# The last layer by Strassen's scheme: low halves on VectorE, split first weights kept in DRAM, squares shared otherwise

## The chip, the cores and the metric

One core of a Trainium2 chip. The metric is the device time of one execution in microseconds, the median of several. Engines: PE (TensorE, matmul), DVE (VectorE), ACT (ScalarE), POOL (GpSimd); SP (SyncE) issues most DMAs, POOL the gathers.

## The reference

Linear attention feeds a mixture of experts, which feeds a last layer. Only the last layer is touched by the change: 2304 tokens of 512 features, 2048 hidden features, a squared relu between two matrices. Its weights come as 64-bit floats.

```python
def _moe2_ref(x, w_in, w_out):
    h = np.maximum(x @ w_in, 0.0)
    return (h * h @ w_out).astype(np.float32)

def reference(**kwargs):
    ...
    attn_out = _attn_ref(**attn_kwargs)
    x = np.ascontiguousarray(attn_out.transpose(0, 2, 1, 3)).reshape(B * S, H * D)
    x = _moe_ref(x=x, **moe_kwargs)
    return _moe2_ref(x=x, **moe2_kwargs)
```

## The kernel before

Instructions run on each engine in the order in which the code records them; a semaphore wait holds up whatever stands behind it on the same engine or queue.

**Split numbers.** A 32-bit operand is split into a high half (ACT copies it to the matmul's type `FR`) and a low half (operand minus high half), and a product is three matmuls: high by high, high by low, low by high.

**The last layer** runs over three blocks (`m`) of six tiles of 128 tokens, 768 tokens each. In a block it runs over 8 sets (`s`) of 256 hidden features; `u = 8 m + s` counts the sets from 0 to 23. In a set, `l_set`:

- The first matrix product is done by Strassen's scheme: tokens are cut in two halves of 384, hidden features in two halves of 128, the 512 inputs in two halves. Seven products (`product(u, p, ...)`, 6 matmuls each of 384 columns) take the place of eight. They use the seven combinations `wa` of the weights and seven combinations `xo` of the tokens. They go in turn into two PSUM banks, M0 and M1, in the order 1, 2, 6, 5, 7, 3, 4. `snap` (ACT) copies a bank to SBUF, `plus` (DVE) adds a snap and a bank, `relu` (ACT) does the last one. The results are c11, c22, c12 and c21, one for each pair of a hidden half `f` and a token half.
- `l_h(u, f, half, c)` makes relu, square and split of one of them into a tile `hq`: before the change relu on ACT (but for c21), the high half as a square on ACT, the full square and the low half on DVE (L1174, L1175).
- `l_2(u, f, half)` multiplies `hq` by the second weights `wo`: nine matmuls of 512 columns, accumulated over the sets of a block in six banks (N0, KV, Tk for token half 0; P, Tq, N1 for half 1). `l_2(u, 0, 0)` ends the set; the other three fill PE's time between the products of the next set (`gap`), so they use the `hq` of the set before.

**The weights.** `a_load` fetches 256 columns of the first weights into one buffer `wr` (512 KB); `a_sums` makes four sums of its quarters on DVE; `a_conv(u)` splits the seven combinations into `wa`: four copies on ACT, four subtractions, on POOL but for u = 0 (L1122). `wa` has two buffers, taken in turn. `o_load` and `o_conv` do the same for the second weights (two loads of 256 KB, L1129; two copies on ACT; two subtractions, on POOL but for u = 0, L1138). All this is done again for each block, though the weights are the same.

**The next block.** In sets 1 to 6 of a block the tokens of the next are made ready: `l_gather` (POOL, two gathers a tile, L1037), `l_sum` (ACT and DVE, L1044, L1045), `l_t` (four PE transposes into M1 within `l_2(u, 0, 0)`, then the ACT copy `xr`, L1056), `x_sum` (DVE, sets 5 to 7), `x_conv` (ACT copy and DVE subtraction of 768 columns; one in set 4, one in set 5, three in set 7, two in set 0).

**Outputs.** At a block's end six banks are copied by `l_out` (ACT, or DVE where `dve` is true) and stored by SP. Tiles n = 3 to 5 of token half 1 are kept back in `OUT` until the first set of the next block (set 8, set 16), where they are copied after the last two `l_h`; in set 9 and 17 the first `l_2` writes bank P again. The loads of the second weights for the next set stand behind these stores in SP's queue.

Of the kernel before, what the change touches and what calls it, by code (L numbers as in the profile page):

```python
# [9 lines left out]
FT = mybir.dt.float32  # L10
FR = mybir.dt.float32r
# [3 lines left out]
AF = mybir.ActivationFunctionType  # L15
# [17 lines left out]
def kernel(  # L33
# [928 lines left out]
    with ExitStack() as ectx:  # L962
# [3 lines left out]
        win_d = dram.tile([DM, F2], FT, name="win_d")  # L966
        wout_d = dram.tile([F2, DM], FT, name="wout_d")
        WIDE = {}

# [138 lines left out]
        def a_sums(u):  # L1108
# [4 lines left out]
            nc.vector.tensor_sub(s[:, 3], a12, s[:, 1])  # L1113

        def a_conv(u):
            a11, a12, a21, a22, s = a_parts(u)
            k = 2 + u % 2
            h, l = [wpb[0].tile([128, 7, 2, 128], FR, name="wa", tag=f"w{k}0{x}") for x in "hl"]
            for c, x in ((slice(0, 2), WR[u][:, :DC, :128].rearrange("p (i c) f -> p i c f", i=2)),
                         (2, a22), (slice(3, 5), s[:, :2]), (slice(5, 7), s[:, 2:])):  # L1120
                nc.scalar.activation(h[:, c], x, AF.Copy)  # L1121
                (nc.gpsimd if u else nc.vector).tensor_sub(l[:, c], x, h[:, c].bitcast(FT))  # L1122
            LW[u] = (h, l)
            del WR[u]
# [7 lines left out]
        def o_conv(u, f):  # L1132
            if f not in WB:
                WB[f] = wpb[0].tile([128, 2, 2, DM], FR, name="wo", tag="w21" + "hl"[f])
            t = WB[f][:, u % 2]
            r = WO[u, f]
            nc.scalar.activation(t[:, 0], r, AF.Copy)  # L1137
            (nc.gpsimd if u else nc.vector).tensor_sub(t[:, 1], r, t[:, 0].bitcast(FT))  # L1138
            WO[u, f] = t
# [25 lines left out]

        def l_h(u, f, half, c, done=False):
            if not done:
                nc.scalar.activation(c, c, AF.Relu)  # L1168
            if f not in HQ:
                pool, tag = ((wpb[0], "w31h"), (ep, "xtl"))[f]  # L1170
                HQ[f] = pool.tile([128, 2, 2, LH], FR, name="hq", tag=tag, bufs=1)
            q = HQ[f][:, half]
            nc.scalar.activation(q[:, 0], c, AF.Square)  # L1173
            nc.vector.tensor_mul(c, c, c)  # L1174
            nc.vector.tensor_sub(q[:, 1], c, q[:, 0].bitcast(FT))  # L1175
            HQ[u, f, half] = q
# [34 lines left out]
        def l_set(u, fill=()):  # L1211
# [19 lines left out]
            due = nxt is not None and 0 < s <= LB  # L1231
            b0, b1 = bank("M0", [128, LH]), bank("M1", [128, LH])
            product(u, 1, b0, True)
            s1 = snap(u, b0, "hh")
# [11 lines left out]
            steps([], [2])  # L1246
            if u + 1 < NU:
                a_sums(u + 1)
# [6 lines left out]
            steps([4], [6])  # L1255
            if u + 1 < NU:
                a_conv(u + 1)
# [13 lines left out]
            product(u, 4, b0, False)  # L1271
            c21 = relu(b0)
            l_h(u, 0, 1, c12)
            l_h(u, 1, 0, c21, True)
            if nxt is not None and s in (NSET - 4, NSET - 3):
                x_conv(nxt, s - NSET + 4)
            for t, n in OUT:
                l_out(t, n, n % 2)
            OUT.clear()
            if nxt is not None and s < LB:  # L1280
                l_gather(nxt * LB + s)
            l_2(u, 0, 0, (lambda: l_t(nxt * LB + s - 1, "M1")) if due else None)
            if u + 1 < NU:
                for f in range(2):
                    o_load(u + 1, f)
            if u + 2 < NU:
                a_load(u + 2)


# [58 lines left out]
        for pt in range(1, NP):  # L1348
# [3 lines left out]
            for f in range(NF):  # L1352
# [34 lines left out]
                if pt == NP - 1:  # L1387
# [17 lines left out]
                    if f == 5:  # L1405
                        x_conv(0, 0)
                        a_load(1)
                    if f == NF - 1:
                        x_conv(0, 4)
                        x_conv(0, 3)  # L1410
                        x_conv(0, 5)
# [112 lines left out]
```

## Time and profile before

| | |
|---|---|
| median of 3 executions | 1069.74 us (1069.7 to 1070.25) |
| the profiled execution | 1078.87 us |
| its span | 1077.0 us |
| mean granted clock of PE | 0.991 |
| last layer in the span | from about 662 us to the end |
| busy in the span | PE 1032.0, DVE 735.5, ACT 578.9, POOL 531.9 us |

Times in the rows are microseconds from the start of the span. A row of a timeline gives start, length, engine, line of the code, instruction, output and inputs by the program's names, shapes, how many were merged, and in brackets how long the engine had stood idle and what ended that. A matmul's end is modelled and overlaps the next one's start. The granted clock is a share of full speed.

### The profile page before, as it was taken

How to read it: one execution, taken by the hardware profiler on the slowest of the kernel's cores; microseconds unless marked ns; L12 is line 12 of the kernel's file. 1: busy time of each engine (PE TensorE's matmuls, PEld its weight loads, DVE VectorE, ACT ScalarE, POOL GpSimd, SP SyncE). 2: the span in 40 equal slices, each digit the busy share in tenths (PEclk: the TensorE clock that was granted, in tenths of full speed). 3: DMA queues.
4: the chain of work that ended last, by engine and by line, in shares of the span. 5: the costliest groups of instructions: out<-in, count | busy, mean ns of one | idle time of the engine just before them, and what ended most of it. 6: DMA issues, size and time to landing. Idle time of an engine off the chain costs nothing.

```text
span 1077.0 us, 19334 instructions
## 1 busy us (share of the span) xinstructions
PE 1032.0 (96%) x7180; PEld 887.6 (82%) x7180; DVE 735.5 (68%) x1434; ACT 578.9 (54%) x1206; POOL 531.9 (49%) x480
## 2 busy tenths in 40 slices
PE   7999999799999999999999999899998999989997
PEld 4776677688989898888898888798887898878996
DVE  5778798632677777786868737766785667866653
ACT  5887777225445353535344426656664655645552
POOL 3444556536546455554545332665555555445340
PEclk9999999899999999999999999999999999999999
DMA  5986533355556656565656342413204232132211
GB/s 148 288 216 204 182 119 111 119 178 186 160 192 199 198 176 206 170 208 184 197 174 203 132 129 82 164 61 117 98 20 158 98 118 70 49 120 76 79 40 61
DMA packets 119141, 153.09 MB, mean 142 GB/s; under 512 B 18306, under 2 KB 71682, under 8 KB 119042
## 3 DMA queue, kind: packets, MB, share of 16 engines
q1 hardware_dynamic: 113282, 132.92, 38.7%
q0 software_dynamic: 5760, 18.88, 5.0%
q8 instruction: 58, 0.95, 0.4%
q14 instruction: 41, 0.34, 0.1%
HBM read 109.22 MB, written 42.54 MB: 141 GB/s over the span
## 4 chain that ended last, share of the span: by engine, by line
PE 71%; DVE 15%; ACT 6%; issue 3%; DMA 2%; another core or an unknown queue 1%; SPq 0%; POOL 0%; ACTq 0%; DVEq 0%
PE M L101 29%; PE N L101 14%; PE KV L101 9%; PE Tq L101 5%; PE P L101 5%; PE Tk L101 3%; DVE c L1174 2%; PE kpair L101 2%; DVE xo L1094 1%; DMA wo<-wout_d 1%; DVE kd L435 1%; DVE kmx L433 1%; DVE c L1158 1%; ACT hq L1173 1%
## 5 line engine op out<-in xcount | busy, mean ns | idle before, releaser
L101 PE MATMUL M<-xo,wa 128*128 128x384 f32 x1008 | 197.0, 339 | 6.8 <-DVE c L1158 3.5
L101 PEld LDWEIGHTS M<-xo,wa 128*128 128x128 f32 x1008 | 178.8, 188 | 21.0 <-DVE c L1158 5.6
L236 ACT ACTIVATE hh<-M 128x304 fp32r<-128x304 f32 (+2 forms) x128 | 48.9, 422 | 225.3 <-PE M L101 204.7
L1122 POOL TENSOR_TENSOR wa<-wr,wa 128x512 fp32r<-128x512 f32 x92 | 117.3, 1305 | 84.7 <-ACT wa L1121 84.3
L1174 DVE TENSOR_TENSOR c<-c 128x384 f32<-128x384 f32 x96 | 76.3, 795 | 95.6 <-ACT hq L1173 95.6
L233 DVE SCALAR_TENSOR_TENSOR hl<-M,hh 128x304 fp32r<-128x304 f32 (+2 forms) x128 | 56.1, 470 | 125.1 <-ACT hh L236 121.6
L515 POOL PARTITION_ALL_REDUCE qmx<-ps x36 | 70.0, 1945 | 80.8 <-ACT ps L513 66.3
L1138 POOL TENSOR_TENSOR wo<-wo 128x512 fp32r<-128x512 f32 x46 | 60.8, 1343 | 94.4 <-ACT wo L1137 94.0
L101 PE MATMUL N<-wo,hq 128*128 128x512 f32 x288 | 83.0, 396 | 0.8 <-DVE hq L1175 0.8
L1175 DVE TENSOR_TENSOR hq<-c,hq 128x384 fp32r<-128x384 f32 x96 | 64.2, 669 | 3.3
L1168 ACT ACTIVATE c<-c 128x384 f32<-128x384 f32 x72 | 37.7, 523 | 50.7 <-DVE c L1158 50.7
L101 PEld LDWEIGHTS N<-wo,hq 128*128 128x128 f32 x288 | 54.0, 189 | 9.7 <-DVE hq L1175 1.2
L1153 ACT ACTIVATE snap<-M 128x384 f32<-128x384 f32 x72 | 34.7, 489 | 48.2 <-PE M L101 48.2
L1158 DVE TENSOR_TENSOR c<-M,snap 128x384 f32<-128x384 f32 x72 | 39.7, 551 | 28.3 <-PE M L101 20.9
L1121 ACT ACTIVATE wa<-wr 128x512 fp32r<-128x512 f32 x96 | 49.4, 569 | 15.8 <-DVE wr L1112 8.9
L1173 ACT ACTIVATE hq<-c 128x384 fp32r<-128x384 f32 x96 | 47.8, 521 | 2.3
L101 PE MATMUL N<-kvc,qp 128*64 128x81 f32 x1024 | 43.9, 238 | 3.9 <-issue 1.7
L101 PEld LDWEIGHTS N<-kvc,qp 128*64 128x64 f32 x1024 | 38.7, 138 | 8.1 <-issue 6.8
L101 PE MATMUL P<-wo,hq 128*128 128x512 f32 x144 | 41.7, 398 | 3.6 <-DVE o L1200 3.6
L1012 POOL TENSOR_TENSOR wx<-wx 128x256 f32<-128x256 f32 x32 | 23.6, 736 | 43.0 <-DVE wx L1008 43.0
L149 POOL TENSOR_TENSOR w30l<-wstage,w30h 128x512 fp32r<-128x512 f32 x16 | 22.7, 1420 | 41.1 <-ACT w30h L148 37.1
L1012 POOL TENSOR_TENSOR wd<-wd 128x256 f32<-128x256 f32 x32 | 23.6, 736 | 37.7 <-DVE wd L1008 37.7
(353 smaller groups left out, 2953.7 us busy)
## 6 DMA issues: line engine op xcount, KB each, us to landing
wstage<-in_moe_w_dram SPq DMA_DIRECT2D x128, 256.0 KB
wr<-win_d SPq DMA_DIRECT2D x24, 512.0 KB
wo<-wout_d SPq DMA_DIRECT2D x48, 256.0 KB
xg_d<-zero SPq DMA_DIRECT2D x8, 1216.0 KB
y_d<-y SPq DMA_DIRECT2D x32, 256.0 KB
wide<-in_moe_w_in_dram SPq DMA_DIRECT2D x32, 256.0 KB
wide<-in_moe_w_out_dram SPq DMA_DIRECT2D x32, 256.0 KB
xg<-xg_d SPq DMA_DIRECT2D x7, 768.0 KB
```

Source lines behind the costliest of these rows:

```text
L101: nc.tensor.matmul(o, l, r, start=start, stop=stop, skip_group_check=True)
L233: nc.vector.scalar_tensor_tensor(hl[:, c0:c1], o, 0.0, hh[:, c0:c1].bitcast(FT), op0=OP.max, op1=OP.subtract)
L236: nc.scalar.activation(hh[:, c[1]:c[2]], c[0], AF.Relu)
L515: nc.gpsimd.partition_all_reduce(mx, ps, 128, bass.bass_isa.ReduceOp.absmax)
L1012: nc.gpsimd.tensor_mul(part, part, exp)
L1121: nc.scalar.activation(h[:, c], x, AF.Copy)
L1122: (nc.gpsimd if u else nc.vector).tensor_sub(l[:, c], x, h[:, c].bitcast(FT))
L1138: (nc.gpsimd if u else nc.vector).tensor_sub(t[:, 1], r, t[:, 0].bitcast(FT))
L1158: nc.vector.tensor_add(c, o, t)
L1173: nc.scalar.activation(q[:, 0], c, AF.Square)
L1174: nc.vector.tensor_mul(c, c, c)
L1175: nc.vector.tensor_sub(q[:, 1], c, q[:, 0].bitcast(FT))
```

## The change

Five things change in the last layer:

- The low halves of both weights (`a_conv`, `o_conv`) are subtracted on DVE in every set; POOL has gathers alone.
- The split first weights of block 0 are stored: after the conversion of set u, SP writes both halves `wa` to a DRAM buffer `wa_d` (`a_store`). In blocks 1 and 2, `a_again` loads them back into the same two buffers; `a_load`, `a_sums` and `a_conv` are left out there.
- `l_h`: for c11 and c22 (`f == half`), ACT does relu, square and the copy to the high half, DVE the low half alone. For c12 and c21 DVE does relu and square in one instruction (max with 0, times c), ACT copies the high half, DVE subtracts.
- The kept-back outputs are copied before the last two `l_h` instead of after, P and N1 by ACT and Tq by DVE (before: P and N1 by DVE, Tq by ACT).
- c21, which is a relu already, goes through the same path as c12.

```diff
+        wa_d = dram.tile([F2 // 256, 2, 128, 7 * 256], FT, name="wa_d")
...
+        def a_tiles(u):
+            LW[u] = [wpb[0].tile([128, 7, 2, 128], FR, name="wa", tag=f"w{2 + u % 2}0{x}") for x in "hl"]
+            return LW[u]
+
+        def a_store(u):
+            for i in range(2):
+                nc.sync.dma_start(wa_d[u, i], LW[u][i].rearrange("p a c f -> p (a c f)").bitcast(FT))
+
+        def a_again(u):
+            for i, t in enumerate(a_tiles(u)):
+                nc.sync.dma_start(t.rearrange("p a c f -> p (a c f)").bitcast(FT), wa_d[u % NSET, i])
...
                 nc.scalar.activation(h[:, c], x, AF.Copy)
-                (nc.gpsimd if u else nc.vector).tensor_sub(l[:, c], x, h[:, c].bitcast(FT))
-            LW[u] = (h, l)
+                nc.vector.tensor_sub(l[:, c], x, h[:, c].bitcast(FT))
...
-            (nc.gpsimd if u else nc.vector).tensor_sub(t[:, 1], r, t[:, 0].bitcast(FT))
+            nc.vector.tensor_sub(t[:, 1], r, t[:, 0].bitcast(FT))
...
-        def l_h(u, f, half, c, done=False):
-            if not done:
-                nc.scalar.activation(c, c, AF.Relu)
+        def l_h(u, f, half, c):
...
             q = HQ[f][:, half]
-            nc.scalar.activation(q[:, 0], c, AF.Square)
-            nc.vector.tensor_mul(c, c, c)
+            if f == half:
+                nc.scalar.activation(c, c, AF.Relu)
+                nc.scalar.activation(c, c, AF.Square)
+            else:
+                nc.vector.scalar_tensor_tensor(c, c, 0.0, c, op0=OP.max, op1=OP.mult)
+            nc.scalar.activation(q[:, 0], c, AF.Copy)
             nc.vector.tensor_sub(q[:, 1], c, q[:, 0].bitcast(FT))
...
+            if NSET <= u + 1 < NU:
+                a_again(u + 1)
             product(u, 1, b0, True)
...
-            if u + 1 < NU:
+            if u + 1 < NSET:
                 a_sums(u + 1)
...
-            if u + 1 < NU:
+            if u + 1 < NSET:
                 a_conv(u + 1)
...
             c21 = relu(b0)
+            for t, n in OUT:
+                l_out(t, n, n % 2 == 0)
+            OUT.clear()
             l_h(u, 0, 1, c12)
-            l_h(u, 1, 0, c21, True)
+            l_h(u, 1, 0, c21)
...
-            for t, n in OUT:
-                l_out(t, n, n % 2)
-            OUT.clear()
...
-            if u + 2 < NU:
+            if u + 2 < NSET:
                 a_load(u + 2)
+            if u + 1 < NSET:
+                a_store(u + 1)
...
                         a_load(1)
+                        a_store(0)
```

DVE in set 2 (sets 1 and 3 read alike), from the weight sums of the next set to the squares of c12 and c21. In the names, `wr` is the raw first weight, `wa` its split form, `ya` a token tile of the next block, `M1` and `M0` the product banks. Before:

```order
L1110 TENSOR_TENSOR wr_8381<-wr_8381 128x256
L1111 TENSOR_TENSOR wr_8381<-wr_8381 128x256
L1112 TENSOR_TENSOR wr_8381<-wr_8381 128x256
L1113 TENSOR_TENSOR wr_8381<-wr_8381 128x256
L1045 SCALAR_TENSOR_TENSOR ya_8356<-yb_8357,gates_79,ya_8356 128x512
L1158 TENSOR_TENSOR c_8465<-M0_8383,snap_8436 128x384
L1174 TENSOR_TENSOR c_8465<-c_8465 128x384
L1175 TENSOR_TENSOR hq_8184<-c_8465,hq_8184 128x384
L1158 TENSOR_TENSOR c_8486<-M1_8384,snap_8428 128x384
L1174 TENSOR_TENSOR c_8486<-c_8486 128x384
L1175 TENSOR_TENSOR hq_8170<-c_8486,hq_8170 128x384
L1174 TENSOR_TENSOR c_8494<-c_8494 128x384
```

The same stretch of DVE now:

```order
L1114 TENSOR_TENSOR wr_8384<-wr_8384 128x256
L1046 SCALAR_TENSOR_TENSOR ya_8359<-yb_8360,gates_79,ya_8359 128x512
L1134 TENSOR_TENSOR wa_8446<-wr_8384,wa_8445 128x512
L1134 TENSOR_TENSOR wa_8446<-wr_8384,wa_8445 128x256
L1134 TENSOR_TENSOR wa_8446<-wr_8384,wa_8445 128x512 x2
L1169 TENSOR_TENSOR c_8470<-M0_8388,snap_8441 128x384
L1188 TENSOR_TENSOR hq_8186<-c_8470,hq_8186 128x384
L1169 TENSOR_TENSOR c_8491<-M1_8389,snap_8433 128x384
L1186 SCALAR_TENSOR_TENSOR c_8491<-c_8491 128x384
L1188 TENSOR_TENSOR hq_8172<-c_8491,hq_8172 128x384
L1186 SCALAR_TENSOR_TENSOR c_8499<-c_8499 128x384
L1188 TENSOR_TENSOR hq_8186<-c_8499,hq_8186 128x384
```

The four subtractions of `wa` stand ahead of the sum c22 (the first `c<-M0`); between c22 and c12 (`c<-M1`) the multiplication is gone; behind c12 a fused relu and square stands before each low half.

DVE at the seam of blocks 0 and 1, from c12 of set 8 to the first sum of set 9 (`o` is an output tile). Before:

```order
L1158 TENSOR_TENSOR c<-M_9267,snap 128x384
L1174 TENSOR_TENSOR c<-c 128x384
L1175 TENSOR_TENSOR hq<-c,hq 128x384
L1174 TENSOR_TENSOR c<-c 128x384
L1175 TENSOR_TENSOR hq<-c,hq 128x384
L1200 COPY o<-P 128x512
L1200 COPY o<-N_8263 128x512
L1158 TENSOR_TENSOR c<-M_9431,snap 128x384
```

And now:

```order
L1169 TENSOR_TENSOR c<-M_9262,snap 128x384
L1213 COPY o<-Tq 128x512
L1186 SCALAR_TENSOR_TENSOR c<-c 128x384
L1188 TENSOR_TENSOR hq<-c,hq 128x384
L1186 SCALAR_TENSOR_TENSOR c<-c 128x384
L1188 TENSOR_TENSOR hq<-c,hq 128x384
L1169 TENSOR_TENSOR c<-M_9413,snap 128x384
```

The copies of P and N1 have gone to ACT, directly behind the relu of c21, and the one copy left on DVE stands ahead of the squares.

SP's queue from the last loads of set 7 to those of set 10 (`wo` second weights, `wr` raw first weights, `wa_d` the DRAM buffer of split first weights). Before:

```order
L1129 DMA wo<-wout_d 128x512 x2
L1100 DMA wr<-win_d 128x4x256
L1209 DMA out_dram<-o 128x512 x6
L1129 DMA wo<-wout_d 128x512 x2
L1100 DMA wr<-win_d 128x4x256
L1129 DMA wo<-wout_d 128x512 x2
```

And now:

```order
L1122 DMA wa_d<-wa 128x1792 x2
L1126 DMA wa<-wa_d 128x1792 x2
L1140 DMA wo<-wout_d 128x512 x2
L1126 DMA wa<-wa_d 128x1792 x2
L1222 DMA out_dram<-o 128x512 x6
L1140 DMA wo<-wout_d 128x512 x2
L1126 DMA wa<-wa_d 128x1792 x2
L1140 DMA wo<-wout_d 128x512 x2
```

A reload of 1.84 MB (two DMAs) stands where a load of 0.5 MB stood; the second weights still stand behind the six outputs.

## Rows read from the trace of the kernel before

**Rows 1.** Page part 1: engine, busy us, share of the span, instructions.
```profile
PE 1032.0 (96%) x7180; PEld 887.6 (82%) x7180; DVE 735.5 (68%) x1434; ACT 578.9 (54%) x1206; POOL 531.9 (49%) x480
```

**Rows 2.** Waits of PE, 660 to 1077: total us, times, longest.
```profile
PE P L101 <- DVE o L1200: 3.6, 2, 1.8
```

**Rows 3.** Windows by set: length, busy PE, PEld, DVE, ACT, POOL, clock, DMA share, GB/s.
```profile
679.10:696.46 17.36, 16.67 (x84) 14.41 (x82) 12.31 (x17) 10.46 (x21) 11.87 (x10) 1.00 0.52 170
712.61:728.75 16.14, 16.14 (x84) 14.52 (x83) 9.79 (x17) 9.49 (x20) 9.48 (x8) 1.00 0.30 102
744.89:761.70 16.81, 16.64 (x83) 14.40 (x82) 13.00 (x21) 9.75 (x20) 9.71 (x8) 1.00 0.28 103
761.70:778.54 16.84, 16.52 (x83) 14.41 (x82) 13.12 (x22) 10.38 (x21) 8.25 (x6) 1.00 0.22 77
778.54:794.25 15.71, 15.71 (x79) 14.14 (x78) 14.03 (x20) 10.07 (x19) 8.69 (x6) 1.00 0.11 41
794.25:811.31 17.06, 16.46 (x79) 13.96 (x78) 13.35 (x20) 11.14 (x22) 8.46 (x6) 1.00 0.22 77
811.31:833.93 22.62, 18.73 (x83) 15.38 (x82) 11.54 (x20) 10.61 (x22) 11.40 (x10) 0.92 0.43 141
948.80:968.76 19.96, 16.49 (x80) 13.91 (x78) 10.75 (x18) 8.70 (x18) 7.48 (x6) 1.00 0.36 119
815.38:819.00 3.62, 3.62 (x9) 2.80 (x10) 1.01 (x2) 0.00 (x0) 0.85 (x1) 0.57 0.71 241
```

**Rows 4.** Timeline of set 3: start, us, engine, line, what [idle before].
```profile
720.22 0.75 DVE L1045 SCALAR_TENSOR_TENSOR ya<-yb,gates,ya 128x512 f32<-128x512 f32 x1 [0.23 <-ACT ya L1044]
720.78 4.86 POOL L1122 TENSOR_TENSOR wa<-wr,wa 128x512 fp32r<-128x512 f32 x4 [3.27 <-ACT wa L1121]
722.24 0.56 DVE L1158 TENSOR_TENSOR c<-M,snap 128x384 f32<-128x384 f32 x1 [1.26 <-PE M L101]
723.38 0.53 ACT L1173 ACTIVATE hq<-c 128x384 fp32r<-128x384 f32 x1
724.54 1.52 DVE L1175 TENSOR_TENSOR hq<-c,hq 128x384 fp32r<-128x384 f32 x1
725.98 0.54 DVE L1158 TENSOR_TENSOR c<-M,snap 128x384 f32<-128x384 f32 x1
727.36 0.94 ACT L1173 ACTIVATE hq<-c 128x384 fp32r<-128x384 f32 x2
728.24 0.60 ACT L1056 ACTIVATE xr<-M 128x512 f32<-128x512 f32 x1
```

**Rows 5.** By line, last layer: count, ns min/median/max, first and last start.
```profile
L1174 DVE TENSOR_TENSOR c<-c x96: 544/559/2331, 674.6 to 1063.9; 128x384 f32<-128x384 f32 x96
L1122 DVE TENSOR_TENSOR wa<-wr,wa x4: 418/684/691, 651.7 to 653.3; 128x512 fp32r<-128x512 f32 x3, 128x256 fp32r<-128x256 f32 x1
```

**Rows 6.** Timeline of the seam between blocks 0 and 1, columns as before.
```profile
814.65 0.68 DVE L1200 COPY o<-P 128x512 f32<-128x512 f32 x1
816.71 1.05 SPq L1129 DMA_DIRECT2D wo<-wout_d  x2
818.15 0.95 POOL L1037 DMA_INDIRECT ya<-y_d,yrows  x1 [8.25 <-DMA out_dram<-o]
820.04 0.63 ACT L1137 ACTIVATE wo<-wo 128x512 fp32r<-128x512 f32 x1 [6.27 <-DMA wo<-wout_d]
822.22 0.63 ACT L1137 ACTIVATE wo<-wo 128x512 fp32r<-128x512 f32 x1 [1.55 <-DMA wo<-wout_d]
823.73 0.86 ACT L1153 ACTIVATE snap<-M 128x384 f32<-128x384 f32 x2
825.23 0.72 ACT L1044 ACTIVATE ya<-ya,gates 128x512 f32<-128x512 f32 x1 [0.65 <-DMA ya<-y_d,yrows]
```

**Rows 7.** Timeline of PE, set 6: product 2 waits.
```profile
763.26 1.31 PE L101 MATMUL M<-xo,wa 128*128 128x384 f32 x6 [0.32 <-ACT xr L1056]
```

**Rows 8.** A window of 2 us at the start of set 2, columns as in rows 3.
```profile
696.00:698.00 2.00, 2.00 (x12) 1.91 (x11) 1.58 (x3) 1.50 (x4) 0.00 (x0) 1.00 1.05 374
```

More of the change, by code (lines that the diff above doesn't have):

```diff
@@ L1113, in a_sums @@
             nc.vector.tensor_sub(s[:, 3], a12, s[:, 1])
+        def a_tiles(u):
[7 more added lines that the diff above has]
+                nc.sync.dma_start(t.rearrange("p a c f -> p (a c f)").bitcast(FT), wa_d[u % NSET, i])
         def a_conv(u):
             a11, a12, a21, a22, s = a_parts(u)
-            k = 2 + u % 2
-            h, l = [wpb[0].tile([128, 7, 2, 128], FR, name="wa", tag=f"w{k}0{x}") for x in "hl"]
+            h, l = a_tiles(u)
             for c, x in ((slice(0, 2), WR[u][:, :DC, :128].rearrange("p (i c) f -> p i c f", i=2)),
```

## The prediction

> **What bounds the kernel now.** I read the page first: TensorE (PE) is busy for 96% of the span [rows 1], so the end can move only where PE waits. The waits of the last layer come next: PE waits there, twice for 1.8 us, for an output copy of VectorE (DVE) [rows 2]. The third view cuts the last layer at the first matmul of each set [rows 3]; it carries the argument. There are 24 sets, 8 for each of three blocks of tokens. An undisturbed set lasts 16.14 us where it carries four transposes for the next block (sets 1 to 6 and 9 to 14) and 15.71 us elsewhere. What exceeds that is lost: 1.22 us in set 1, 0.67 and 0.70 in sets 5 and 6, 1.35 in set 8, 6.48 in set 9, 4.25 in set 17. Sets 13, 14 and 16 repeat 5, 6 and 8 to a hundredth or two. Together that is 10.4 + 4.25 + 2.7 = 17.4 us, the most that this change can win. The other sets lose nothing worth a row, so faster helpers win nothing in them.
>
> Why sets lose: in set 3 (no loss) one subtraction of DVE takes 1.52 us and ends 0.42 us after the group of four on GpSimd (POOL), which ends at 725.64 [rows 4]; instructions of this size have a median of 0.56 and a longest of 2.33 [rows 5]. So DVE is held up while POOL works. At the seam from block 0 to block 1, PE waits until DVE has copied bank P at 815.33, since the copies stand behind four squares and subtractions; SyncE (SP) issues the next second weights only behind the last output, at 816.71; ScalarE (ACT) stands before their conversion until 820.04 and again until 822.22, and the snap that frees PE's bank starts at 823.73 [rows 6]. After PE's wait of 1.80 us the granted clock is 0.57 over 3.62 us [rows 3], between the upper level (2.4 GHz) and the lower (1.2 GHz): 3.62 x 0.43 = 1.6 us more.
>
> **The change part by part.** *POOL's subtractions leave.* Then DVE's instructions of 384 columns stay at 0.56 us. In set 3 that takes 1.52 - 0.56 = 0.96 us out between the sum c22 (722.24) and the sum c12 (725.98) [rows 4].
>
> *They go to DVE.* The second weights' two (0.68 us each, as in [rows 5]) fall where DVE waits for ACT's chain on c11; their cover is that DVE is busy 9.79 of 16.14 us [rows 3]. The first weights' four cost 3 x 0.684 + 0.418 = 2.47 us [rows 5], in sets 0 to 6 only, and stand just ahead of c22. There DVE idled 1.26 us [rows 4], and neighbours overlap by some 0.1 (two squares take 0.94 us, not twice 0.53), so c22 comes 0.8 us later (bounds 0.4 and 1.2). With the 0.96 won, c12 comes at 725.8, as good as before.
>
> *The chain behind c12.* Before: two squares on ACT, end 728.30, then the copy `xr` that frees bank M1 [rows 4]. Now DVE squares c12, ACT copies, DVE subtracts, DVE squares c21, ACT copies, in this order, and `xr` stands behind the second copy. With 0.56 for each of DVE's four steps, 0.53 for the copies, 0.03 for a hand-over (722.24 + 0.56 and so on to 723.38) and 0.60 for `xr`, less overlaps, `xr` ends 3.8 us after c12's sum starts: 729.55. Set 4 starts at 728.75 and its product 2 wants M1 1.05 later, at 729.80. Slack 0.25 us. The fused square has no row; its nearest are 0.56, a product of 384 columns [rows 5], and 0.75, a fused one of 512 [rows 4]. I take 0.56 for the size; at 0.75 the slack is gone.
>
> Where ACT has a conversion of 768 columns (some 0.8 us) between, in sets 4 and 5, `xr` is 0.75 later; in sets 5 and 6 DVE also has four block sums of 256 columns (0.42 each [rows 5]) ahead of c22. Product 2 then waits 0.5 us in set 5, 1.2 in set 6 and 0.5 in set 7. Each wait also costs PE a restart: with 0.32 of waiting [rows 7] set 6 lost 0.70, part of it elsewhere; I add 0.2. Sum 2.8 us against 1.37 now. Set 1, where second weights and gather land late and a store of 1.84 MB is new in the queue, loses 1.5 against 1.22. Set 0 gains a subtraction at 0.56 and pays the four on DVE: zero, between -0.8 and +0.6.
>
> *Blocks 1 and 2 load the split weights.* Gone from each set: four sums, four ACT copies, the four subtractions. c22 has nothing ahead of it, c12 starts as product 3 ends, and `xr` has 0.5 us of slack; behind a conversion it misses by 0.2. Sets 13 and 14 lose 0.4 each instead of 0.7. Each set reloads 2 x 128 x 1792 x 4 bytes = 1.84 MB. SP issues it as soon as the products of the set before are through, so it has a set's length. The queue moved 374 GB/s in a full stretch [rows 8]: 5 us. In set 1 it moved 170: 11 us [rows 3]. Both fit; I price it at zero. Behind SP's wait for PE stand only the second weights, due a set later.
>
> *The seams.* The three held-back outputs come ahead of the last two squares, P on ACT. Product 4 ends some 13.7 us into set 8 (15.71 less nine matmuls, 3.62 x 0.57); after the relu of c21 and one copy, 0.6 us or so each, P is free at 14.9, ahead of PE's need in set 9: the wait of 1.80 us is gone, and the clock's 1.6 with it. SP issues the second weights at 16.3 instead of 22.5 us after set 8's start; with 3.33 us to land [rows 6] ACT starts 3.9 us into set 9, the second 2.2 later at worst, and with relu, square and copy the snap is taken at 8.8; product 7 wants it at 8.4. That loses 0.4, and as much again if the gather (issued at 818.15, landed at 825.23; now issued near 812) holds up the sum ahead of c22: set 9 loses 0.8, set 17, without a gather, 0.3. Sets 8 and 16 lose nothing: DVE has no weight sums and no stretched subtractions there.
>
> On this gather: before, it landed 7.1 us after its issue with 1 MB of weights beside it; now 1.84 MB stand in SP's queue before it. In order of issue it would wait 5 us or more for them, and set 9 would lose 3 to 4; no row here tells whether it does. The Trainium skill (DMA: Bandwidth & Descriptors, "Queues, rings and completion order") states that each DMA engine alternates between the queue rows it has work for; by that the gather shares and set 9 stays near 0.8.
>
> **Sum.** Now 17.4. After: set 1 1.5, sets 5 to 7 2.8, set 9 0.8, sets 13 and 14 0.8, set 17 0.3, together 6.2. Gain 11.2 us of the profiled 1078.87, that is 1.04%; of the median 1069.74 that leaves **1058.6 us**. The profiled execution is 0.9% above the median; I assume that waits scale with it.
>
> **The rivals.** *B, the longer chain:* `xr` is half a microsecond later than summed. Then sets 3 and 4 wait too (0.45 each), the four late ones of block 0 and three of block 1 wait 0.5 more: +4.4, **1063**. For it: a slack of 0.25. Against: nearly every part has a row.
>
> *C, the seam half mended:* the 1.80 waits go, but weights or gather land as late as before, behind six outputs and the reload: set 9 keeps 6.48 - 1.80 - 1.6 = 3.1, set 17 2.45: +4.5, **1063**, up to 1066 with the gather in order of issue.
>
> *E, DVE is not held up by POOL:* then the 0.96 stays, and c12 costs some 0.9 us in six sets of block 0 and 0.6 in six of block 1: +9, **1068**, not to be told from no change. Against: the long subtraction ends with POOL's group. The Trainium skill (GPSIMD Engine Reference, "Specifications") says that POOL shares its SBUF interfaces with DVE and contends with instructions of two SBUF inputs; the trace agrees (2.33 us at most against 0.56).
>
> *D, slower:* the reloads miss their set. A set of block 1 moves 1.84 + 0.52 (second weights) + 0.52 (gather) = 2.88 MB in 16.14 us, so below 178 GB/s PE waits at product 1. At 155 GB/s, between sets 1 and 9 (170 and 141 [rows 3]), each of 8 sets would take 18.6 us: +19.6 - 11.2, **1078**. It outweighs the gain below 163 GB/s. Against: those sets had less to move, and 374 was reached.
>
> **How the numbers follow.** Forecast 0.62 (own spread 1054 to 1061.5: all but 1.5 us of the loss won at best, the slack gone at worst), B 0.16, C 0.14, E 0.04, D 0.04. Range 1053.5 to 1065: it takes in B and most of C and leaves out E, D and the tails. A measurement of this kernel tells 0.2% (2.1 us): faster 0.92, same 0.04, slower 0.04.
>
> **What would show it.** Right: no arithmetic on POOL in the last layer, DVE's 384 columns at 0.56 throughout, sets 8 and 16 at 15.7, set 9 near 17, set 17 near 16, no wait of PE for an output copy, waits for `xr` in sets 5 to 7. B shows as waits for `xr` in sets 3 and 4, C as ACT idle for second weights over 3 us, D as PE waiting for the reload. Wrong altogether if sets that lose nothing now lengthen.

## Result and profile after

The changed kernel takes 1060.6 us (median of 4 runs, 1059.99 to 1061.37), the kernel before 1069.72 (4 runs, 1068.85 to 1070.25). The ratio is 0.9916, with a 95% interval from 0.9899 to 0.9933: 9.1 us or 0.85% faster. The forecast was 1058.6, in a range from 1053.5 to 1065.

The profiled execution took 1060.74 us, with a span of 1059.0. The page's line of busy times, which answers to [rows 1]:

```profile
PE 1024.3 (97%) x7180; PEld 884.9 (84%) x7180; DVE 672.9 (64%) x1394; ACT 563.8 (53%) x1168; POOL 352.9 (33%) x342
```

DVE, ACT and POOL all have less to do. The waits of PE from 640 us on answer to [rows 2]; the columns after the colon are the sum, the count and the longest:

```profile
PE M L101 <- ACT xr L1057: 3.9, 7, 1.0
PE M L101 <- DVE c L1169: 1.9, 1, 1.9
PE Tk L1055 <- DVE ya L1046: 0.3, 1, 0.3
```

Before, beside the 3.6 us for the output copies, the larger waits were:

```profile
PE M L101 <- DVE c L1158: 3.5, 8, 1.3
PE M L101 <- ACT snap L1153: 2.3, 2, 1.5
PE M L101 <- ACT xr L1056: 0.7, 2, 0.3
```

No output copy is among the waits now: both of 1.8 us at the seams are gone, and so are those for a snap and all but one for a sum c. In their place stand seven waits for `xr`, the copy that frees bank M1, where there were two. Where they fall is read from the windows by set, which answer to [rows 3] (set 0, 1, 2, 4, 5, 6, 8, 9, 10 and 17; the number behind the stretch is its length, the third from the end the granted clock):

```profile
653.28:671.00 17.72, 15.66 (x72) 13.47 (x71) 15.24 (x27) 13.99 (x26) 0.00 (x0) 0.90 0.26 83
671.00:687.60 16.60, 16.58 (x84) 14.41 (x82) 9.45 (x20) 9.70 (x19) 6.50 (x7) 1.00 0.87 324
687.60:704.85 17.25, 16.42 (x84) 14.48 (x83) 11.23 (x22) 10.26 (x21) 1.90 (x3) 1.00 0.59 227
720.98:737.12 16.14, 16.14 (x83) 14.52 (x82) 10.28 (x20) 10.17 (x21) 1.63 (x2) 1.00 0.57 214
737.12:753.92 16.80, 16.42 (x83) 14.48 (x82) 12.31 (x25) 10.61 (x21) 0.00 (x0) 1.00 0.43 157
753.92:771.41 17.49, 16.45 (x84) 14.49 (x83) 12.78 (x26) 10.80 (x21) 0.00 (x0) 1.00 0.56 214
787.70:803.40 15.70, 15.70 (x79) 14.14 (x78) 7.73 (x14) 10.80 (x20) 0.00 (x0) 1.00 0.39 155
803.40:820.27 16.87, 16.84 (x84) 14.32 (x82) 7.14 (x14) 8.11 (x16) 6.26 (x7) 1.00 0.95 341
820.27:837.52 17.25, 16.42 (x84) 14.48 (x82) 7.84 (x14) 8.41 (x17) 1.89 (x3) 1.00 0.42 162
934.56:950.27 15.71, 15.71 (x80) 14.14 (x78) 7.44 (x14) 7.39 (x15) 0.00 (x0) 1.00 0.70 248
```

Sets 8 and 17 lose nothing, set 9 0.73 instead of 6.48. Sets 2 and 10, which lost nothing before, lose 1.11 each, sets 5 and 6 0.66 and 1.34, and set 0 is 1.12 longer. The table gives all kernels of this study, one profiled execution of each: the length of set 0, and for the others what they lose over 16.14 or 15.71 us (sets left out lose under 0.3). Each number is worked out from the starts of the sets in that kernel's trace. The last column is the time from the start of set 0 to the end. Up to 1.5 us of set 0 is chance (last section).

| kernel | set 0 | 1, 2 | 5 to 7 | 8 | 9 | 10 | 13 to 15 | 16 | 17 | 0 to end |
|---|---|---|---|---|---|---|---|---|---|---|
| before | 16.60 | 1.23 | 1.37 | 1.35 | 6.48 | 0 | 1.38 | 1.36 | 4.25 | 414.5 |
| before_again | 16.61 | 0.95 | 1.37 | 1.34 | 6.59 | 0 | 1.36 | 1.36 | 4.33 | 414.3 |
| changed | 17.72 | 1.57 | 2.59 | 0 | 0.73 | 1.11 | 1.07 | 0 | 0 | 405.7 |
| after_again | 16.16 | 3.02 | 2.58 | 0 | 0.05 | 1.13 | 1.04 | 0 | 0.09 | 404.8 |
| only_low_on_dve | 17.72 | 0 | 0.16 | 0 | 5.90 | 0 | 0.16 | 0 | 5.06 | 409.6 |
| lows_and_outputs | 17.62 | 0.09 | 0.14 | 0 | 1.24 | 0 | 0.15 | 0 | 0 | 400.1 |
| outputs_behind | 17.71 | 1.30 | 2.58 | 0 | 4.52 | 1.13 | 1.04 | 0 | 5.81 | 414.8 |
| no_reload | 17.70 | 0 | 2.58 | 0.06 | 1.01 | 1.11 | 2.59 | 0.06 | 0.24 | 406.2 |
| squares_paired | 16.14 | 1.99 | 0.17 | 0 | 0 | 0 | 0 | 0 | 0 | 399.1 |
| sum_behind_c22 | 17.69 | 1.03 | 1.17 | 0 | 0 | 0 | 1.04 | 0 | 0 | 401.6 |
| three_edits | 15.88 | 2.85 | 0 | 0 | 0 | 0 | 0 | 0 | 0 | 399.0 |
| old_squares_sum_behind | 16.16 | 0 | 0 | 0 | 0.44 | 0 | 0 | 0 | 0.28 | 397.6 |
| old_squares_set0_pool | 16.59 | 0 | 0 | 0 | 0.93 | 0 | 0 | 0 | 0.25 | 398.0 |
| paired_no_reload | 17.69 | 0 | 0 | 0 | 0.62 | 0 | 0 | 0 | 0 | 399.1 |

The kernel before took 1069.6 us beside the first four experiments and 1079 beside the other eight. Times are therefore compared as ratios within a group, and columns of the last layer across groups.

### The profile page after: what moved, and what is told of

Its sections match the earlier page's. It is cut to its first block, busy times and chain, and to the rows that moved or that the text cites. A ratio compares the mean times of both kernels' runs of the same rounds, so it can differ in the third digit from the quotient of the medians.

```text
span 1059.0 us, 19130 instructions
## 1 busy us (share of the span) xinstructions
PE 1024.3 (97%) x7180; PEld 884.9 (84%) x7180; DVE 672.9 (64%) x1394; ACT 563.8 (53%) x1168; POOL 352.9 (33%) x342
## 4 chain that ended last, share of the span: by engine, by line
PE 77%; DVE 11%; ACT 6%; DMA 3%; issue 1%; SPq 0%; POOL 0%; DVEq 0%; ACTq 0%; POOLq 0%
PE M L101 32%; PE N L101 15%; PE KV L101 9%; PE Tq L101 6%; PE P L101 6%; PE Tk L101 3%; DMA yb<-y_d,yrows 2%; PE kpair L101 2%; DVE kd L435 1%; ACT hq L1187 1%; DVE kmx L433 1%; DVE wa L1134 1%; DVE hq L1188 1%; PE qpair L101 1%; PE M L207 1%
## 5 line engine op out<-in xcount | busy, mean ns | idle before, releaser
L1188 DVE TENSOR_TENSOR hq<-c,hq 128x384 fp32r<-128x384 f32 x96 | 53.6, 559 | 86.3 <-ACT hq L1187 86.3
L1038 POOL DMA_INDIRECT ya<-y_d,yrows x18 | 18.4, 1024 | 194.5 <-PE M L101 82.7
L1187 ACT ACTIVATE hq<-c 128x384 fp32r<-128x384 f32 x96 | 50.3, 524 | 34.8 <-DVE c L1186 33.2
L1183 ACT ACTIVATE c<-c 128x384 f32<-128x384 f32 x48 | 25.2, 524 | 60.6 <-DVE c L1169 60.6
L101 PE MATMUL Tk<-wo,hq 128*128 128x512 f32 x144 | 42.1, 400 | 0.0
L101 PE MATMUL KV<-wo,hq 128*128 128x512 f32 x144 | 41.3, 395 | 0.0
L101 PE MATMUL Tq<-wo,hq 128*128 128x512 f32 x144 | 40.9, 392 | 0.0
L776 POOL DMA_INDIRECT xg_d<-x,slots x32 | 33.1, 1035 | 12.1 <-issue 4.8
```

Source lines behind the costliest of these rows:

```text
L101: nc.tensor.matmul(o, l, r, start=start, stop=stop, skip_group_check=True)
L776: st = nc.gpsimd.indirect_dma_start(out=xg_d, out_offset=bass.IndirectOffsetOnAxis(ap=slots[:, T0[g] + i, c:c + 1], axis=0), in_=src, in_o ...
L1038: nc.gpsimd.indirect_dma_start(out=y, out_offset=None, in_=y_d[:YA_ROWS] if t < LB else y_d, in_offset=bass.IndirectOffsetOnAxis(ap=yrows[ ...
L1187: nc.scalar.activation(q[:, 0], c, AF.Copy)
```

## Is the gain in the last layer?

The two first profiles stand 18 us apart, the medians 9. So the kernel before was profiled again, unchanged.

> The kernel before, unchanged. My theory: the 9 us by which the profiled execution of the kernel before stood above its median lay ahead of the last layer (there set 0 began at 662.5 us, in the changed kernel at 653.3) and were chance; then set 0 begins near 653.5 here, the profile's span is near 1068, the last layer to the start of the last second-layer stretch takes 400.8 again, and the losses by set are those of the first profile to 0.2 us each. Rival: the change also shortens the stretch ahead of the last layer; then set 0 begins at 662 again and the median is near 1078. The time against itself: 1069.7, ratio 1.000 within 0.2%.

Measured: 1069.92 us, ratio 1.0007 (0.9998 to 1.0017). Set 0 began at 653.16, the span was 1067.5, and the last layer lost what it had lost before (table). The extra 9 us of the first profile lie ahead of it, nearly all around one stretch; the first row is the first profile of the kernel before, the second the one taken again:

```profile
204.00:224.00 20.00, 15.66 (x92) 13.99 (x91) 8.89 (x53) 1.34 (x5) 11.25 (x21) 0.83 0.43 155
```
```profile
204.00:224.00 20.00, 18.77 (x122) 16.37 (x121) 9.93 (x49) 4.62 (x13) 9.86 (x19) 1.00 0.51 178
```

In the first, PE ran 92 matmuls there at a granted clock of 0.83, in the second 122 at 1.00, the upper level. "Chance" was not the whole of it: in each later group all seven runs of the kernel before lay near 1079, so this is a level that can hold for a whole group, and the first profile was taken on it. The groups also ran on three different chips, so whether the level goes with the chip stays open. The last layer is the same on both: 414.5 and 414.3 us. The changed kernel's 405.7 and 404.8 say that the gain, 9.2 us on the mean, is all there.

## One part alone: the low halves on DVE

```diff
-                (nc.gpsimd if u else nc.vector).tensor_sub(l[:, c], x, h[:, c].bitcast(FT))
+                nc.vector.tensor_sub(l[:, c], x, h[:, c].bitcast(FT))
...
-            (nc.gpsimd if u else nc.vector).tensor_sub(t[:, 1], r, t[:, 0].bitcast(FT))
+            nc.vector.tensor_sub(t[:, 1], r, t[:, 0].bitcast(FT))
```

> The kernel before with one part of the change alone: all low halves of the first and second weights on VectorE, none on GpSimd. My theory (GpSimd's arithmetic held VectorE up): the subtractions of 384 columns fall from 0.67 to 0.56 us on the mean, none is over 1 us, which pays for the four subtractions of weights (2.5 us a set) now ahead of c22; sets 5, 6, 13, 14 keep their 0.7 each, the seams keep 6.5 and 4.3: 1069.7, between 1067 and 1072. Rival E (VectorE isn't held up by GpSimd): the mean stays at 0.67 and c12 comes 0.8 us later in the sets of the first two blocks; the slack of the old chain takes part of it: 1073 or more.

Measured: 1064.55 us, ratio 0.9942 (0.9919 to 0.9964): 5 us faster, outside what I had expected and on the other side of rival E. DVE's subtraction of 384 columns, in the kernel before (first row) and here (second row; minimum, median and longest in ns):

```profile
L1175 DVE TENSOR_TENSOR hq<-c,hq x96: 557/558/1532, 666.5 to 1055.1; 128x384 fp32r<-128x384 f32 x96
```
```profile
L1175 DVE TENSOR_TENSOR hq<-c,hq x96: 557/558/565, 666.7 to 1050.1; 128x384 fp32r<-128x384 f32 x96
```

No stretched instruction is left (the longest multiplication fell from 2.33 to 0.61 us), so rival E falls: POOL's arithmetic did hold DVE up. And sets 1, 5, 6, 8, 13, 14 and 16 give back nearly all that they lost, 6.4 us by the table, though DVE has more to do (in set 3 it is busy 11.34 us instead of 9.79). The seams keep 5.9 and 5.1. The Trainium skill (GPSIMD Engine Reference, "Specifications") says that POOL contends with DVE's instructions of two SBUF inputs; the rows agree, and show how far: 1.53 us against 0.56.

## One part undone: the order of the outputs

```diff
-            for t, n in OUT:
-                l_out(t, n, n % 2 == 0)
-            OUT.clear()
             l_h(u, 0, 1, c12)
             l_h(u, 1, 0, c21)
             if nxt is not None and s in (NSET - 4, NSET - 3):
                 x_conv(nxt, s - NSET + 4)
+            for t, n in OUT:
+                l_out(t, n, n % 2)
+            OUT.clear()
```

> The changed kernel with one part undone: the held-back output copies stand again behind the last two squares of the set, with the old share of the engines. My theory (the order of the copies is what mended the seams): PE waits for an output copy again, 1.8 us at each seam, the granted clock falls behind each wait, and the second weights are asked for 6 us later; set 9 loses 6 us or so, set 17 4.2: 1060.6 + 5.6 + 4.2 = 1070, between 1067 and 1071. Rival: the seams were mended because GpSimd, the block sums and the conversions left them; then the order is worth little, set 9 loses under 3 us and set 17 under 1.5, and the time is below 1064.

Measured: 1070.59 us, ratio to the kernel before 1.0005 (0.9996 to 1.0015): without the order, nothing is left of the gain. Its waits of PE from 650 us on:

```profile
PE M L101 <- ACT snap L1164: 5.3, 2, 2.9
PE M L101 <- ACT xr L1057: 3.9, 7, 1.0
PE M L101 <- DVE c L1169: 2.1, 2, 1.9
PE P L101 <- DVE o L1213: 1.9, 2, 0.9
```

The waits for the output copy are 0.9 here, not 1.8, as with the low halves alone (1.0); the larger part, 5.3, is the snap behind the late second weights. So the order works through two routes, as the prediction had it, and the second is the dearer one. Sets 9 and 17 lose 4.52 and 5.81 here, 0.73 and 0 with the order. Of the granted clock, which I had expected to fall behind each wait, only set 17 shows a fall (0.92; set 9 1.00).

## One part undone: store and reload

All three blocks load and split the plain weights; `a_store` and `a_again` are not called.

```diff
-            if NSET <= u + 1 < NU:
-                a_again(u + 1)
...
-            if u + 1 < NSET:
+            if u + 1 < NU:
                 a_sums(u + 1)
...
-            if u + 1 < NSET:
+            if u + 1 < NU:
                 a_conv(u + 1)
...
-            if u + 2 < NSET:
+            if u + 2 < NU:
                 a_load(u + 2)
-            if u + 1 < NSET:
-                a_store(u + 1)
...
-                        a_store(0)
```

> The changed kernel with one part undone: nothing of the split first weights is stored or reloaded; all three blocks load the plain weights, form the block sums and split them, on ScalarE and VectorE. My theory: sets 13 and 14 lose 2.6 together with set 15 as sets 5 to 7 do now, instead of 1.1, and the sums and conversions stand ahead of c22 in sets 8 to 22 as well; against it set 1 may win 0.4 without the store, and the gathers of block 1 share the DMA queues with less, so sets 9 and 10 lose 1 us instead of 1.8: 1062, between 1060.5 and 1065. Rival (the reload costs as much as it saves, because the gather waits beside it): no difference from 1060.6 or faster, with sets 9 and 10 under 1 us.

Measured: 1060.36 us, ratio to the kernel before 0.9919 (0.9896 to 0.9942), no difference from the changed kernel's 1060.6, the rival's time. But the sum is made of two parts that cancel. Sets 1, 2 and 13 to 15 here:

```profile
670.56:686.71 16.15, 16.15 (x84) 14.53 (x83) 10.42 (x21) 9.88 (x20) 6.02 (x7) 1.00 0.69 219
686.71:702.85 16.14, 16.14 (x84) 14.52 (x83) 10.28 (x20) 10.18 (x21) 1.89 (x3) 1.00 0.31 98
868.14:884.94 16.80, 16.42 (x84) 14.48 (x82) 12.32 (x25) 10.61 (x21) 0.00 (x0) 1.00 0.19 63
884.94:902.40 17.46, 16.42 (x83) 14.49 (x82) 12.74 (x26) 10.80 (x21) 0.00 (x0) 1.00 0.18 61
902.40:918.72 16.32, 16.00 (x79) 14.11 (x78) 12.67 (x24) 11.02 (x21) 0.00 (x0) 1.00 0.10 32
```

Sets 13 to 15 lose 2.59, as sets 5 to 7 do, instead of 1.07: the reload saves 1.5 there. Sets 1 and 2 lose nothing instead of 1.57: the store costs that. With it in the queue the gather of set 1 lands late, and DVE, which sums the gathered rows ahead of c22, stands still. In the changed kernel's set 1:

```profile
680.26 0.75 DVE L1046 SCALAR_TENSOR_TENSOR ya<-yb,gates,ya 128x512 f32<-128x512 f32 x1 [2.56 <-DMA yb<-y_d,yrows]
680.93 2.22 DVE L1134 TENSOR_TENSOR wa<-wr,wa 128x512 fp32r<-128x512 f32 x4
683.07 0.55 DVE L1169 TENSOR_TENSOR c<-M,snap 128x384 f32<-128x384 f32 x1
```

Sets 9 and 10 lose 1.01 and 1.11 here, where I had expected 1 us together and the rival less. The gather is in time (DVE starts its sum at 811.27 without having waited for it), but the four subtractions of first weights, 2.22 us, now stand ahead of c22 in its place. So the loss at the seam is not the reload's alone.

## Two parts without the new squares

The kernel before with the low halves on DVE (diff above) and

```diff
             c21 = relu(b0)
+            for t, n in OUT:
+                l_out(t, n, n % 2 == 0)
+            OUT.clear()
             l_h(u, 0, 1, c12)
             l_h(u, 1, 0, c21, True)
             if nxt is not None and s in (NSET - 4, NSET - 3):
                 x_conv(nxt, s - NSET + 4)
-            for t, n in OUT:
-                l_out(t, n, n % 2)
-            OUT.clear()
```

> The kernel before with two parts of the change: all low halves on VectorE, and the held-back output copies ahead of the last two squares; the squares stay shared as before, nothing is reloaded. My theory (the new sharing of the squares lengthens the chain to the copy that frees bank M1 and costs some 5 us, the reload is worth nothing): the losses are those of the kernel with the low halves alone but with the seams mended: set 0 1.1 more than before, sets 6 and 14 0.2 each, sets 9 and 17 1 and 0.3 instead of 5.9 and 5.1: 1054.5, between 1053 and 1057, which beats the changed kernel by 6 us. Rival (the outputs can come first only because the new squares take ScalarE's two squares at the end of the set away): here c21's and c12's squares hold up product 1's snap, sets 9 and 17 lose 3 us each: 1059 or more.

Measured: ratio 0.9866 (0.9849 to 0.9882) to the kernel before, 1065.09 us where that took 1079.12; 400.1 us from set 0 to the end, 5.6 less than the changed kernel. It is well ahead of the changed kernel, whose ratio was 0.9916 and later 0.9919. So one part of the change, the new sharing of the squares, costs some 6 us: 406.2 without the reload against 400.1, two kernels that differ in the squares alone.

## The chain behind c12, and the sum ahead of c22

The first kernel changes the order within the last two squares alone; what it replaces are the two calls of `l_h`, which did square, copy and subtraction one after the other for c12 and then for c21.

```diff
-            l_h(u, 0, 1, c12)
-            l_h(u, 1, 0, c21)
+            pair = []
+            for f, half, c in ((0, 1, c12), (1, 0, c21)):
...
+                nc.vector.scalar_tensor_tensor(c, c, 0.0, c, op0=OP.max, op1=OP.mult)
+                nc.scalar.activation(q[:, 0], c, AF.Copy)
+                pair.append((q, c))
+            for q, c in pair:
+                nc.vector.tensor_sub(q[:, 1], c, q[:, 0].bitcast(FT))
```

> The changed kernel with the steps behind c12 and c21 in another order: both fused squares of VectorE first, then both copies of ScalarE, then both subtractions, so the copy that frees bank M1 comes about 1.06 us earlier (0.55 of a square and 0.59 of waiting drop out). My theory (that copy is late, and it alone costs sets 2, 5 to 7, 10, 13 and 14): their waits for it, 3.9 us in all, and the 0.2 that each adds go: sets 5 to 7 and 13 to 14 lose under 0.5 together instead of 3.7, sets 2 and 10 0.3 instead of 1.1 each; set 0, 1 and 9 stay: 1055.5, between 1054.5 and 1057.5. Rival (the late point is VectorE's queue ahead of c22, not the chain behind c12): the sets keep over half of it, 1058.5 or more.

Measured: ratio 0.986 (0.9844 to 0.9877), 1064.03 us where the kernel before took 1079.12; 399.1 us from set 0 to the end, 6.6 less than the changed kernel. No wait for `xr` is left; these are all waits of PE from 650 us on:

```profile
PE M L101 <- DVE c L1169: 3.4, 2, 1.9
PE Tk L1055 <- DVE ya L1046: 0.3, 1, 0.3
```

Sets 5 to 7 and 13 to 15 lose 0.17 together instead of 3.66, sets 2 and 10 nothing. The rival falls: the late point was the chain. The changed kernel's chain in set 5 shows it:

```profile
751.60 0.55 DVE L1169 TENSOR_TENSOR c<-M,snap 128x384 f32<-128x384 f32 x1
752.19 0.56 DVE L1186 SCALAR_TENSOR_TENSOR c<-c 128x384 f32<-128x384 f32 x1
753.34 0.56 DVE L1188 TENSOR_TENSOR hq<-c,hq 128x384 fp32r<-128x384 f32 x1 [0.59 <-ACT hq L1187]
753.81 0.55 DVE L1186 SCALAR_TENSOR_TENSOR c<-c 128x384 f32<-128x384 f32 x1
```

DVE waits 0.59 for ACT's copy and subtracts before it squares c21. In the paired order the second square fills that wait.

The second kernel leaves the chain and moves DVE's sum of gathered rows:

```diff
             if due:
-                l_sum(nxt * LB + s - 1)
+                ya, yb = YA[nxt * LB + s - 1]
+                nc.scalar.activation(ya, ya, AF.Copy, scale=gates[:, nxt * LB + s - 1, 0:1])
...
             c22 = plus(b0, s5)
+            if due:
+                nc.vector.scalar_tensor_tensor(ya, yb, gates[:, nxt * LB + s - 1, 1:2], ya, op0=OP.mult, op1=OP.add)
```

> The changed kernel with VectorE's sum of the gathered rows (0.75 us, which waits for the gather) put behind the sum c22 instead of ahead of it; ScalarE's scaling stays. My theory (the gather lands late at the seam, since it shares the queues with the reload, the second weights and two more gathers, and holds up c22 through VectorE's queue; in set 1 the store does the same): set 9 loses 0.4 or less instead of 0.73, set 10 nothing instead of 1.11, sets 1 and 2 under 0.5 together instead of 1.57, and sets 5 to 7 about 1.0 instead of 2.6, since the sum falls where VectorE waits 1.7 us for ScalarE: 1056.3, between 1055 and 1058.5. Rival (the second weights, which land late too, cost sets 9 and 10): these keep 1.5 of their 1.84.

Measured: ratio 0.9882 (0.9865 to 0.9898), 1066.28 us; 401.6 us from set 0 to the end, 4.1 less than the changed kernel. Sets 9 and 10:

```profile
810.42:826.57 16.15, 16.15 (x84) 14.53 (x82) 8.26 (x15) 8.46 (x17) 6.93 (x7) 1.00 0.96 348
826.57:842.71 16.14, 16.14 (x84) 14.52 (x82) 6.79 (x12) 8.20 (x17) 1.89 (x3) 1.00 0.47 180
```

They lose nothing, instead of 0.73 and 1.11, at the same load of the queues (0.96 of the DMA engines' time against 0.95). So nearly all of the 1.84 us at the seam was the gather, reaching PE through DVE's order and then through the chain. The second weights, the rival, account for some 0.2: in the changed kernel's set 9 the snap behind them started 7.94 us into the set and product 7 at 8.47, here 7.36 and 8.37. (The paired squares leave nothing of the seam either, but there the gather's sum started 10.94 us into set 9 instead of 11.68, so only the 1.11 of set 10 can be put down to them.) In the changed kernel one sees the hold-up in set 9 and, seven microseconds later, PE's wait for `xr` in set 10:

```profile
815.08 0.75 DVE L1046 SCALAR_TENSOR_TENSOR ya<-yb,gates,ya 128x512 f32<-128x512 f32 x1 [3.04 <-DMA yb<-y_d,yrows]
815.74 0.55 DVE L1169 TENSOR_TENSOR c<-M,snap 128x384 f32<-128x384 f32 x1
```
```profile
822.32 1.31 PE L101 MATMUL M<-xo,wa 128*128 128x384 f32 x6 [0.83 <-ACT xr L1057]
```

Sets 5 to 7 came out at 1.17, near the 1.0 expected; set 2 kept 1.02, where I had expected under 0.5.

## Set 0, and all edits together

The third edit, besides the two above, is

```diff
-                nc.vector.tensor_sub(l[:, c], x, h[:, c].bitcast(FT))
+                (nc.gpsimd if u == 1 else nc.vector).tensor_sub(l[:, c], x, h[:, c].bitcast(FT))
```

> The changed kernel with the paired squares, the sum behind c22, and, third, the four subtractions of the first weights in set 0 alone back on GpSimd, as before the change. My theory (in set 0 those four stand ahead of c22 and cost it 1.1 us): set 0 takes 16.6 us again instead of 17.7, sets 1 to 17 lose under 1.2 together instead of 7.0: 1053.5, between 1052.5 and 1055.5. Rival (set 0 is longer for another reason, the store or the squares): set 0 stays at 17.7, 1054.6.

Measured: ratio 0.9857 (0.984 to 0.9874), 1063.48 us; 399.0 us from set 0 to the end, no less than with the paired squares alone. Sets 0 and 1:

```profile
662.76:678.64 15.88, 14.28 (x70) 12.00 (x69) 12.77 (x19) 13.43 (x25) 5.70 (x4) 1.00 0.10 37
678.64:697.62 18.98, 16.72 (x82) 14.48 (x83) 11.90 (x25) 9.92 (x21) 6.94 (x7) 1.00 0.92 326
```

Set 0 fell by 1.8 us, more than expected: the granted clock did not fall in it, as it had in the first profile of the changed kernel (last section). Set 1 took it back: 2.84 us over 16.14. It waits for the gather, which is issued after set 0 and shares the queue with the store. ACT scales the gathered rows ahead of the first weights' copies, so c22 still hangs on it. So far as these profiles show, set 0's loss and the store's are one loss: what is saved in the one, the other takes.

The changed kernel was then run again beside three others:

> The changed kernel, unchanged, as the measure for the other three. Both theories: from set 0 to the end 405.7 us by its profile, against 414.4 of the kernel before, so 8.7 to 9.1 us faster than that on whichever level the stretch ahead of the last layer has here (set 0 has begun at 653 and at 662 us).

Measured: 1069.91 us where the kernel before took 1078.98, ratio 0.9919 (0.9902 to 0.9935); 404.8 us from set 0 to the end. It shows the same trade without an edit: set 0 took 16.16, sets 1 and 2 lost 3.02; sets 0 to 2 took 51.46 us, in the first profile 51.57.

The other three drop the store, and with it the reload. First, lows_and_outputs with DVE's sum behind c22 (the same edit as above):

> The kernel before with the low halves on VectorE, the outputs ahead of the last two squares (squares shared as before, no reload), and VectorE's sum of the gathered rows behind c22. My theory (set 9's rest of 1.24 us is that sum, waiting for the gather): set 9 loses under 0.2, sets 6 and 14 at most 0.2 each, set 0 17.6 us; from set 0 to the end 398.9 us, 6.8 less than the changed kernel, 15.5 less than the kernel before. Rival (the second weights are as late as the gather): set 9 keeps 0.6 or more, 399.6.

Measured: ratio 0.9857 (0.984 to 0.9873), 1063.4 us; 397.6 us from set 0 to the end. Sets 6 and 14 lose nothing; set 9 keeps 0.44, between theory and rival. The trace shows neither cause: the second weights are in time (product 7 starts 8.37 us into the set), and DVE's sum of the gathered rows is behind c22, which starts at 12.02, held up by the four subtractions of first weights (2.23 us). The 1.3 us under the expectation are set 0, which took 16.16 here; that is luck, since the clock did not fall in it. Then the same with set 0's subtractions on POOL:

> The kernel with the old squares, the outputs ahead and the sum behind c22, and in set 0 alone the four subtractions of the first weights on GpSimd. My theory (what set 0 loses by them, set 1 would have lost to the gather, which is issued a fixed time after set 0 ends): set 0 takes 15.9 to 16.6 us instead of 17.6, set 1 takes at least half of that back; without the store in the queue it takes less back than in the changed kernel: 398.0 us from set 0 to the end, between 397.3 and 398.9. Rival (set 0's 1.1 us are a loss of its own): 397.3 or less.

Measured: ratio 0.9852 (0.9835 to 0.9868), 1062.51 us: 16.5 us less than the kernel before and 7.4 less than the changed kernel beside it. It is the lowest ratio of all, though not clear of the next ones (0.9857). From set 0 to the end it takes 398.0 us, as expected, but not for the reason given: set 1 took nothing back (16.15), and set 9 lost 0.93. Between it and the kernel without this edit no difference can be told.

Last, the paired squares and the sum behind c22 without store and reload:

> The changed kernel with the paired squares and the sum behind c22, and without store and reload (all blocks load and split the plain weights). My theory (with the chain short, the reload has nothing left to save, and the store only delays the gather of set 1): sets 2 to 22 lose under 0.5 together, sets 0 and 1 take 33.8 instead of 34.2 to 34.9: 398.7 us from set 0 to the end, no worse than with the reload (399.0). Rival (the reload carries part of the gain once the chain is short): sets 13 to 15 lose 1 us or more, 400 or more.

Measured: ratio 0.9874 (0.9858 to 0.989), 1064.56 us; 399.1 us from set 0 to the end. Sets 13 to 15 lose nothing, so the rival falls: with a short chain the reload saves nothing there. Set 9 keeps 0.62, a little over the 0.5 expected for all sets from 2 on.

## Why the prediction was right, and which terms were off

*What bounds the kernel, and the seams:* right. The loss was 17.4 us, and most sets that lost nothing still lose nothing. Set 7 now loses 0.58, as forecast; sets 2 and 10 lose 1.11 each, which was not, and lengthened sets were the prediction's own sign of being wrong altogether. It was wrong there by 2.2 us (see set 9). The output waits went, SP issues the second weights 16.4 us after set 8's start (forecast 16.3), and sets 8 and 16 take 15.7.

*The low halves:* the mechanism was right, and larger than its place in the sum. Alone, this part makes the kernel 5 us faster. In set 3 c22 comes 0.79 us later with this part alone and c12 0.18 earlier, as I had summed (0.8 and 0.2); what I had not argued is that it frees all of sets 5, 6, 13 and 14.

*The chain behind c12:* right to a tenth where it was summed. The fused square took 0.56, the value taken, and `xr` ended 3.8 us after c12's sum began (in set 1, 685.80 to 689.60). Sets 5 to 7 lost 2.59 (forecast 2.8), sets 13 to 15 1.07 (0.8); sets 3 and 4 lost nothing, so rival B didn't come. What the sum did not show is that this part is a cost: compared with the kernel before, whose own chain was stretched by POOL, it looked like 0.9 us (3.6 against 2.7 in sets 5 to 7 and 13 to 15); compared with the old squares on quiet engines it is 6.

*Set 9:* the step that failed. Of its two terms of 0.4 the second weights' was some 0.2 in the first profile and nothing in the second. The gather's I priced by how late c22 comes, and stopped at the set's end. The lateness passes on through c12 and `xr` to product 2 of set 10: 1.84 us in sets 9 and 10 together (1.18 in the second profile) instead of 0.8. Set 2 is the same; that sets 1 and 2 together came to the 1.5 forecast for set 1 alone is luck. Rival C did not come: no more than this was left of the seam.

*The gather beside the reload:* not decided. The second half of the gather landed 8.5 us after its issue in the first profile of the changed kernel (806.58 to 815.08) and 7.8 in the second. That is later than an even share would give (an estimate: 0.52 MB at half of the 356 GB/s that were moved from 804 to 816 us, 3 us), and set 9 lost 0.73 and 0.05, which is less than I expected of order of issue. Without the reload the same half had landed by 6.5 us after its issue (804.73 to 811.27), so the reload delayed it by 1.3 us at least. The Trainium skill's rule that engines alternate between queue rows (DMA: Bandwidth & Descriptors, "Queues, rings and completion order") is neither shown nor refuted: from 804 to 816 us POOL's queue moved 1.05 MB and SP's 3.22, with work for both most of the time.

*Set 0:* forecast zero, between -0.8 and +0.6; measured +1.12 in one profile and -0.44 in the other. The wait for c22 was there both times (1.94 and 1.92 us); only what the clock did after it differed (below).

*Set 17:* 0.3 us forecast, 0 and 0.09 measured.

*The sum:* 6.2 us of loss were forecast. Measured were 1.57, 2.59, 1.84 and 1.07 in sets 1 to 15, 7.1 in all, and 1.1 more in set 0: 8.2 in the first profile (7.5 in the second). The 2 us above 6.2 are as much as lies between the forecast and the result, but the sum also had no term for the tail: from the start of set 23 to the end the changed kernel takes 30.16 and 29.97 us, the kernel before 29.45 and 29.41, and the difference lies behind PE's last matmul; why is open. Rival D never came near: the reload landed in 5.2 us (median), and PE waited for it nowhere. The assumption that waits scale with the profiled 1078.87 was empty: those 9 us were not in the last layer.

## To carry to other kernels

An instruction that waits for a transfer should not stand in an engine's order ahead of what the bottleneck needs next: moving one sum of 0.75 us behind c22 mended two sets. Where steps hop from one engine to another and back, two such chains should be interleaved rather than run one after the other; here that was worth some 6 us. What a part of a change is worth is told best by taking or undoing it alone: of four parts one was worth 5 us, one 10, one nothing, and one cost 6.

## What the hardware did that was not expected

The same wait of PE is followed by a lower granted clock in one execution and not in the other. After the wait of 1.94 us in set 0 of the changed kernel, and of 1.92 in its second profile, the rest of the set reads (first and second profile):

```profile
666.23:671.00 4.77, 4.77 (x16) 4.11 (x17) 2.83 (x6) 2.55 (x6) 0.00 (x0) 0.64 0.93 290
```
```profile
676.15:679.38 3.23, 3.23 (x16) 2.84 (x17) 1.88 (x4) 1.93 (x5) 0.00 (x0) 1.00 0.98 311
```

The same 16 matmuls took 4.77 us at 0.64, between the lower level (1.2 GHz) and the upper (2.4 GHz), and 3.23 at the upper: 1.54 us that no edit decides. Such a stretch lies in set 0 of seven of the ten traces in which PE had waited 1.9 us there for c22. A difference of set 0 in one pair of profiles is thus no evidence on an edit; the 9 us between the two levels of the whole kernel hang together with a lower clock too: in the slower of the two profiles of the kernel before PE waits 4.3 us for a routing mask of DVE (1.3 in the other), and the clock around the end of that wait is 0.59 from 212 to 220 us (1.00 in the other). What begins it is open.
